# Six more q and k transposes on the DMA queue, and a new order of loads, in a fused attention and feed-forward kernel

## Chip, cores and metric

One NeuronCore of a Trainium2 chip. The metric is the device time of one execution in microseconds; the median of several runs is compared.

## The reference

```python
# q, k, v: (4 batches, 8 heads, 768 tokens, 64); n_sink = 4, window = 128
scores = q @ k.T / sqrt(64)
keep = (key position < n_sink) | (0 <= query position - key position < window)
a = softmax(where(keep, scores, -1e9))
x = (a @ v) with the heads side by side           # (3072 tokens, 512)
out = ((x @ w1) * (x @ w2)) @ w3 @ w_out          # 512 -> 1024 -> 1024 -> 512, float32 out
```

## The kernel before

The 3072 tokens are four batches of 768; each batch is six blocks of 128 tokens, in two halves ("chunks") of three blocks. Matrix products run in bf16 with float32 sums.

Since nothing nonlinear stands between w3 and w_out, the kernel first multiplies these two into one matrix w3o ("the fold"): TensorE transposes w3 (L349 and L380), and multiplies by w_out (L357 and L387). The first three row blocks of w3 are folded together, the other five one by one.

Attention for a batch goes through these steps. Loads bring q, k and v in by blocks of 128 tokens, 128 KB each, issued by GpSimd, which turns float32 into bf16 on the way (L159). q and k must stand with the head dimension on the partitions, so they are transposed into qkT, which has two buffers, one for even and one for odd batches. For batch 0 and batch 1 TensorE transposes (L437 and L460), into a PSUM tile mm, and ACT or DVE copies it to qkT (L142). For batches 2 and 3 the DMA engines transpose, issued by SP (L484), one instruction for one block of q or of k. Then TensorE computes scores (L585, and L523 for the four sink tokens), ACT takes the exponential (L603), DVE multiplies by a mask (L609), TensorE multiplies by v (L661, tile av), and DVE divides by the sum of weights (L671 and L676), into xs. xs is transposed once more into xT: on TensorE for batches 0 and 1 (L697), by DMA for batches 2 and 3 (L717).

The feed-forward part runs by halves of 384 tokens. For each of eight column blocks there are two gate products of four matmuls each (L741, one with w1 and one with w2, 384 columns), a copy of the first (L142, a_sb) and a multiplication with the second (L756, ab). Then the product with w3o (L771), a copy to o_sb (three buffers), and a store of 128 rows (L788, issued by SP).

The program's order is set at build time by a planner in the kernel (L792 on). Each step is an Op with an engine, an assumed duration, dependencies and a priority; the planner takes for each engine the step that can start soonest, and among those that can start at once the one with the lowest priority number. `when` (L425) gives attention steps their priority from LEAD and SPREAD; FOLD_J and FOLD_I give that of the fold. Idle places that the planner sees on TensorE in the first 45 us are filled with matmuls on zeros (L850, 104 of them). On the chip each engine then runs its own list strictly in this order, and waits only on semaphores. GpSimd takes the loads in the order of the string LOADS (L241), with eight outstanding at most.

The buffer `big` holds w3 and w_out, and later q and k of batches 2 and 3; so those loads come after the fold. The planner further orders the loads of batch 3 behind transposes of batch 2 and behind one another; DEEP says how many of them may be ahead. What it orders so on GpSimd is a place in time in the plan, not a semaphore on the chip. In SP's list, transposes of batch 3 stand behind those of xs of batch 2, by ORDER (L472).

Memory of PSUM: two wide tiles sc for scores, one av, three mm. The mm tiles serve gate products, output products and the transposes on TensorE alike.

Of the kernel before, what the change touches and what calls it, by code (L numbers as in the profile page):

```python
# [21 lines left out]
def kernel(  # L22
# [23 lines left out]
    NP = H // 2  # L46
    NB = S // P
    NC = 2
    QC = NB // NC
# [32 lines left out]
    qN = {0: early[0], 1: near[0]}  # L82
    kN = {0: early[1], 1: near[1]}
    for b in (2, 3):
        o = (b - 2) * 2 * NQ
# [36 lines left out]
    TUS = 1.3  # L122
# [14 lines left out]
    PE, ACT, DVE, POOL, SP = "pe", "act", "dve", "pool", "sp"  # L137
# [3 lines left out]
    def copy(out, in_):  # L141
        (nc.scalar.copy if turn_of[0] == ACT else nc.vector.tensor_copy)(out, in_)  # L142

    def cols(n, k=1):
        return k * (n / 2400.0 + 0.0025)

    def act_us(n):
        return 0.165 + n / 1200.0

    def dve_us(n, x=1.0):  # L150
        return 0.15 + n / 960.0 / x
# [12 lines left out]
    def pool_op(us, fn, deps=()):  # L164
        return Op(POOL, us, fn, deps)

    KA, LEAD, SPREAD = 3, 0, 0.9
    FOLD_J, FOLD_I = 0.5, 1010
    DEEP, ORDER = 2, 1
    FUSED = (1, 2, 3)  # L170
    KINDS = (0, 2, 2, 2)
    QK_BY_DMA = (2, 3)
    X_BY_DMA = ((2, 0), (2, 1), (3, 0), (3, 1))

    def load_w3(i):
# [15 lines left out]
    def load_qk(dst, src, b, c, h0, h1):  # L191
        return load(POOL, dst[b][:, c, h0:h1, :],
                    src[b, h0:h1, c * TOK:(c + 1) * TOK, :].rearrange("h (p j) d -> p h (j d)", j=QC),
                    (h1 - h0) * TOK * D * 4, QC * D * 4)
# [35 lines left out]
    got = {}  # L230
# [5 lines left out]
    for r in range(2):  # L236
# [2 lines left out]
            got["kq"[n], 0, 0, r] = cast((DVE, ACT)[n], 0.5, dst[0][:, 0, 2 * r:2 * r + 2, :],  # L239
                                         first_home[i][:, 0:TOK].rearrange("p (h m) -> p h m", h=2), st[i])  # L240
    LOADS = """k0-0-4 v0-0 ident q0-0-4 pick w3j-2-4 v0-1 tri v0-2 w3j-0-1 w3j-4-6 w3j-1-2 wo-1-2 wo-0-1  # L241
        wo-2-4 w3j-6-8 wo-4-6 w3-6 wo-6-8 w3-5 w3-4 q0-1-0 w3-7 k0-1-0 v0-5 w0 v0-3 v0-4 w3 k1-5
        q1-3 w2 w1 k1-4 w3-3 q1-1 k1-3 q1-4 q1-0 q1-5 k1-2 q1-2 v1-4 k1-0 q2-1 k1-1 q2-0 q2-2 k2-1
        q3-5 q2-3 v1-2 v1-1 v1-0 k2-2 k2-0 v2-4 v1-5 v2-0 k2-3 q3-2 v2-1 v1-3 v3-1 q2-5 v2-2 k2-5
        q2-4 k2-4 q3-4 k3-3 v3-2 v3-3 k3-5 v3-5 v3-0 v2-5 q3-3 k3-2 k3-4 v2-3 k3-1 q3-0 k3-0 v3-4
        q3-1"""

    def masks(part):
        m = maskt[:, 0, :].rearrange("p (k q) -> p k q", q=P)
# [27 lines left out]
    for key in LOADS.split():  # L277
        n = [int(x) for x in key[2 if key[:2] == "wo" else 3 if key[:3] == "w3j" else 1:].split("-") if x.isdigit()]
# [10 lines left out]
        elif key[:2] == "wo" or key[:3] == "w3j":  # L289
            o = (load_wo if key[1] == "o" else load_w3j)(*n)  # L290
# [13 lines left out]
        elif key[0] in "kq":  # L304
            _, c, h0 = n
            o = load_qk(kN if key[0] == "k" else qN, k if key[0] == "k" else q, 0, c, h0, h0 + (H if c else H // 2))
# [14 lines left out]
    def transposed(home_ap, n):  # L321
        return home_ap[:].bitcast(BF16)[:, 0:n]
# [8 lines left out]
    acc_keys, n = [], 0  # L331
# [80 lines left out]
    xt_ready, chunk_dep = {}, {}  # L412
# [3 lines left out]
    for b in range(B):  # L416
        kind = KINDS[b]
        T = qkT_home[b % 2]
        war = []
        if b >= 2:  # L420
            war = list(all_sc[b - 2])
        tp_of = {}
        base = 10 * b

        def when(part, early):  # L425
            return 1000 + 200 * (b - 1) + LEAD + 200 * SPREAD * part if b else early
        if b == 0:
            for c in range(NC):
                for r in range(NP):
                    x = []  # L430

                    def tps(b=b, c=c, r=r, x=x):
                        tp = transposed(x[0].slot["mm"], 6 * P).rearrange("p (s j m) -> p s j m", s=2, m=P)
                        for s, src in ((0, kN[b]), (1, qN[b])):
                            for j in range(QC):
                                for e in range(2):
                                    nc.tensor.transpose(tp[64 * e:64 * e + 64, s, j, :],  # L437
                                                        src[:, c, 2 * r + e, j * D:(j + 1) * D], ident[:])

                    def tpc(T=T, c=c, r=r, x=x):  # L440
                        tp = transposed(x[0].slot["mm"], 6 * P).rearrange("p (s j m) -> p s j m", s=2, m=P)
                        for s in range(2):
                            copy(
                                T[:, r, s, c * TOK:(c + 1) * TOK].rearrange("p (m j) -> p m j", j=QC),
                                tp[:, s, :, :].rearrange("p j m -> p m j"))
                    a = Op(PE, cols(P, 6) + 0.12, tps, [got["k", b, c, r], got["q", b, c, r], op_ident],
                           base + 1 + r * 0.1, takes=["mm"])
                    x.append(a)
                    tp_of[c, r] = Op(EITHER, (2 * act_us(3 * P), 2 * dve_us(3 * P)), tpc, [a],
                                     base + 1, frees=[(a, "mm")])  # L450
        elif b not in QK_BY_DMA:
            for c in range(NC):
                for r in range(NP):
                    x = []

                    def tps(b=b, c=c, r=r, x=x):
                        tp = transposed(x[0].slot["mm"], 6 * P).rearrange("p (s j m) -> p s j m", s=2, m=P)
                        for s, src in ((0, kN[b]), (1, qN[b])):
                            for j in range(QC):
                                nc.tensor.transpose(tp[:, s, j, :],  # L460
                                                    src[:, QC * c + j, r * P:(r + 1) * P], ident[:])

                    def tpc(T=T, c=c, r=r, x=x):
                        copy(
                            T[:, r, :, c * TOK:(c + 1) * TOK],
                            transposed(x[0].slot["mm"], 6 * P).rearrange("p (s m) -> p s m", s=2))
                    a = Op(PE, cols(P, 6), tps,
                           [got[n, b, QC * c + j] for n in "kq" for j in range(QC)] + [op_ident] + war,
                           when((r / 4 + c) / 2 - 0.1 if kind != 1 else r / 4 + c / 50 - 0.1, 0), takes=["mm"])
                    x.append(a)  # L470
                    tp_of[c, r] = Op(EITHER, (act_us(6 * P), dve_us(6 * P, 2)), tpc, [a], base + 1, frees=[(a, "mm")])
        if ORDER and b == 3 and 2 in QK_BY_DMA:  # L472
            for c in range(NC):
                if (2, c) in X_BY_DMA:
                    for (s_i, kb), o in tp_of.items():
                        if kb // QC == c:
                            o.after = chunk_dep[2, c][1][-1]
        if b not in QK_BY_DMA:
            tdep = lambda c, r: [tp_of[c, r]] + ([tp_of[0, r]] if c else [])
        else:  # L480
            for kb in range(NB):
                for s, n, src in ((0, "k", kN), (1, "q", qN)):
                    def dmt(b=b, s=s, src=src, kb=kb, T=T):
                        nc.sync.dma_start_transpose(out=T[:, :, s, kb * P:(kb + 1) * P], in_=src[b][:, kb, :])  # L484
                    tp_of[s, kb] = Op(SP, TUS, dmt, [got[n, b, kb]] + war, base)
                    tp_of[s, kb].turn, tp_of[s, kb].pitch = 1.1, TUS
            if b + 1 in QK_BY_DMA:
                seen = []
                for o in in_big:
                    if o.batch == b:  # L490
                        seen.append(next(t for t in tp_of.values() if o in t.deps))
                    elif o.batch == b + 1:
                        o.deps += seen[:-3]
                behind = [o for o in in_big if o.batch == b + 1]
                for o, p in zip(behind[DEEP:], behind):
                    o.deps.append(p)
            tdep = lambda c, r: [tp_of[s, kb] for s in range(2) for kb in range(3 * c + 3)]

        def sk(b=b, T=T):
            for e in range(2):  # L500
# [16 lines left out]
        for q0, q1 in groups:  # L517
# [21 lines left out]
            o = Op(ACT, act_us(w), sse, [a], base + 2, frees=[(a, "mm")])  # L539
# [22 lines left out]
        for n_v, visit in enumerate(visits):  # L562
# [26 lines left out]
            if sinks:  # L589
                sinks[2].append(s_)  # L590
                o = Op(ACT, act_us(sinks[3]), sinks[1], [s_], base + 2, frees=[(s_, "mm")])
# [237 lines left out]
    with tc.manual_schedule():  # L829
        left, lanes = len(ops), []  # L830
        while left:
# [5 lines left out]
            start, e, o = min(moves, key=lambda x: (x[0], x[1]))  # L837
# [4 lines left out]
            if e == PE and start < 45.0 and start - free[PE] > 0.12:  # L842
                one = cols(P) * (2 if free[PE] < WARM else 1)
                n = min(24, int((start - free[PE] - 0.05) / one))
# [9 lines left out]
            for i, n in enumerate(o.takes):  # L854
                f, s = rings[n].soonest()
# [74 lines left out]
```

## Time and profile before

| | us |
|---|---|
| median of four runs | 200.03 |
| the runs | 199.15, 200.17, 204.35, 199.89 |
| the profiled execution | 199.15 |
| its span, first to last instruction | 197.4 |
| TensorE busy | 192.3 |
| VectorE (DVE) busy | 112.0 |
| ScalarE (ACT) busy | 103.8 |
| GpSimd (POOL) busy, nearly all of it issuing loads | 73.1 |
| mean TensorE clock granted | 1.0 |

The page gives the busy time of each engine, then the span in 40 slices of some 4.9 us: a digit is the busy share in tenths. The chain of waits follows the last instruction back to what released it. Rows of groups give line, engine, operation, output <- input, number, and the shortest, median and longest duration in ns. In rows by time the columns are start, duration, engine, line, operation and count; several instructions that follow one another are put together in one row. In rows by stretches, the busy time of PE, the weight loads (PEld), DVE, ACT and POOL follow the length, then the granted clock, a DMA share and GB/s. DMA issued by SP shows there with the time it takes SP, not with the time until its data has landed.

### The profile page before, as it was taken

To read this page: it belongs to the slowest core of one execution; us is meant where nothing else is said; L and a number is where in the kernel's file an instruction comes from. 1 tells how busy PE (TensorE), PEld (TensorE's weight loads), DVE (VectorE), ACT (ScalarE), POOL (GpSimd) and SP (SyncE) were. 2 spreads that over 40 slices of the span, in tenths; PEclk is the share of its full clock that TensorE was granted. 3 is DMA by queue.
4 is the path that set the end of the run, shared out by engine and by line. 5 is a ranking of instruction groups with operands and counts; after the bars stand their busy time and mean duration, and the time that the engine had idled before them with its cause. 6 is when DMAs were issued, how large, how long until landed. Compare 5 with 4: busy or idle time off the path is not lost.

```text
span 197.4 us, 4573 instructions
## 1 busy us (share of the span) xinstructions
PE 192.3 (97%) x1840; PEld 118.0 (60%) x1840; DVE 112.0 (57%) x255; ACT 103.8 (53%) x165; POOL 73.1 (37%) x96
## 2 busy tenths in 40 slices
PE   7999999999999999999999999999999999999993
PEld 6776656567566546566665546654666665555442
DVE  3976507696356757866897704544698654223200
ACT  3683548754539567837456623335884433343233
POOL 7997547677998556535363000000000000000000
PEclk9999999999999999999999999999999999999999
DMA  6999999999999999999999965351202142020133
GB/s 173 173 184 193 202 190 183 181 193 165 155 154 138 155 181 183 207 167 185 142 155 157 139 180 178 67 107 56 106 3 45 34 134 56 2 106 3 53 129 137
DMA packets 98181, 26.42 MB, mean 134 GB/s; under 512 B 86896, under 2 KB 94576, under 8 KB 98160
## 3 DMA queue, kind: packets, MB, share of 16 engines
q0 software_dynamic: 73584, 14.29, 91.4%
q1 hardware_dynamic: 23888, 11.38, 26.4%
q10 hardware_dynamic: 688, 0.46, 0.7%
q8 instruction: 14, 0.23, 0.5%
q14 instruction: 7, 0.06, 0.1%
HBM read 29.39 MB, written 6.29 MB: 181 GB/s over the span
## 4 chain that ended last, share of the span: by engine, by line
PE 92%; DMA 3%; POOL 2%; ACT 1%; issue 1%; DVE 0%; POOLq 0%; DVEq 0%
PE mm L741 43%; PE mm L771 21%; PE av L661 8%; PE sc L585 6%; PE mm L387 4%; DMA big<-in_moe_w_dram 3%; PE sc L357 2%; PE mm L460 1%; PE mm L697 1%; PE mm L380 1%; PE mm L357 1%; PE mm L523 1%; POOL early L159 1%; PE mm L349 1%; PE av L850 1%
## 5 line engine op out<-in xcount | busy, mean ns | idle before, releaser
L741 PE MATMUL mm<-xT,w_sb 128*128 128x384 bf16 x512 | 90.3, 326 | 0.0
L741 PEld LDWEIGHTS <-w_sb 128*128 128x128 bf16 x512 | 47.7, 98 | 31.4 <-issue 1.8
L756 DVE TENSOR_TENSOR ab<-a_sb,mm 128x384 bf16<-128x384 f32 x64 | 35.4, 553 | 32.2 <-PE mm L741 27.7
L603 ACT ACTIVATE ex<-sc 128x1024 bf16<-128x1024 f32 (+2 forms) x49 | 44.0, 941 | 5.9 <-PE sc L585 4.3
L771 PE MATMUL mm<-w3o,ab 128*128 128x512 bf16 (+2 forms) x208 | 45.0, 363 | 0.0
L142 ACT COPY a_sb<-mm 128x384 f32<-128x384 f32 x53 | 25.3, 478 | 36.1 <-PE mm L741 18.2
L609 DVE TENSOR_TENSOR am<-ex,maskt 128x1024 bf16<-128x1024 bf16 (+2 forms) x49 | 30.1, 623 | 4.7 <-ACT ex L603 4.5
L771 PEld LDWEIGHTS <-ab 128*128 128x128 bf16 x208 | 18.8, 98 | 19.0 <-issue 0.6
L142 ACT COPY o_sb<-mm 128x512 f32<-128x512 f32 (+2 forms) x21 | 11.4, 545 | 25.7 <-PE mm L771 25.7
L159 POOL DMA_DIRECT2D vN<-in_v_dram x24 | 21.1, 884 | 6.8 <-DMA big<-in_k_dram 3.5
L661 PEld LDWEIGHTS <-am 128*128 128x128 bf16 x352 | 17.0, 97 | 3.5 <-issue 0.3
L661 PE MATMUL av<-vN,am 128*128 128x65 bf16 x352 | 19.0, 194 | 0.0
L676 DVE TENSOR_TENSOR xs<-av,rec 128x384 bf16<-128x384 f32 x32 | 17.7, 554 | 0.6
L671 DVE RECIPROCAL rec<-av 128x6 f32<-128x6 f32 x32 | 6.2, 194 | 16.6 <-PE av L661 16.4
L585 PE MATMUL sc<-qkT 64*128 64x128 bf16 (+1 forms) x248 | 14.7, 241 | 0.1
L159 POOL DMA_DIRECT2D big<-in_k_dram x12 | 10.6, 880 | 9.9 <-PE mm L741 2.9
L661 PE MATMUL av<-vsb,es 128*128 128x130 bf16 x64 | 12.9, 220 | 0.0
L159 POOL DMA_DIRECT2D big<-in_q_dram x12 | 10.6, 882 | 4.5 <-DMA vN<-in_v_dram 2.1
L585 PEld LDWEIGHTS <-qkT 64*128 64x128 bf16 x248 | 8.1, 94 | 5.9 <-issue 4.3
L387 PE MATMUL mm<-big,w3t 128*128 128x512 bf16 x40 | 9.5, 380 | 0.0
L850 PEld LDWEIGHTS <-zeros 128*128 128x128 bf16 x104 | 7.7, 115 | 2.0 <-DVE zeros L219 1.3
L850 PE MATMUL mm<-zeros 128*128 128x128 bf16 x75 | 7.4, 266 | 1.3 <-DVE zeros L219 1.3
(64 smaller groups left out, 143.8 us busy)
## 6 DMA issues: line engine op xcount, KB each, us to landing
out_dram<-o_sb SPq DMA_DIRECT2D x23, 256.0 KB
vN<-in_v_dram POOLq DMA_DIRECT2D x24, 128.0 KB, 10.6
w_sb<-in_moe_w_dram POOLq DMA_DIRECT2D x8, 256.0 KB, 9.8
big<-in_q_dram POOLq DMA_DIRECT2D x12, 128.0 KB, 7.8
big<-in_k_dram POOLq DMA_DIRECT2D x12, 128.0 KB, 10.5
big<-in_moe_w_dram POOLq DMA_DIRECT2D x5, 256.0 KB, 8.9
big<-in_moe_w_out_dram POOLq DMA_DIRECT2D x3, 256.0 KB, 6.4
near<-in_k_dram POOLq DMA_DIRECT2D x6, 128.0 KB, 7.9
```

Of the source, the lines that this page charges most:

```text
L142: (nc.scalar.copy if turn_of[0] == ACT else nc.vector.tensor_copy)(out, in_)
L159: op = Op(eng, us, lambda: (nc.gpsimd if eng == POOL else nc.sync).dma_start(out=out, in_=in_), deps)
L387: nc.tensor.matmul(x[2].slot["mm"][:], x[1].slot["w3t"][:, j, :], wo_sb[:, j, :], start=(j == 0), stop=(j == KFF - 1))
L585: nc.tensor.matmul(sc[:, e, c * P:(c + n) * P], T[hp, r, 0, kb * P:(kb + 1) * P], T[hp, r, 1, qb * P:(qb + n) * P], start=True, stop=True)
L603: nc.scalar.activation(y[1].slot["ex"][:, :, 0:w], y[0].slot[key][:, :, 0:w], ACTF.Exp, scale=scale)
L609: nc.vector.tensor_mul(y[2].slot["am"][:, :, 0:w], y[1].slot["ex"][:, :, 0:w], maskt[:, :, m0:m0 + w].to_broadcast([P, 2, w]))
L661: nc.tensor.matmul(o, lhs, rhs, start=(i == 0), stop=(i == len(todo) - 1), skip_group_check=True)
L676: nc.vector.tensor_mul(xs_first[c].slot["xs"][:, :, r * P:(r + 1) * P].rearrange("p k (e d) -> p k e d", d=D), av_of(x[0].slot["av"])[:, : ...
L741: nc.tensor.matmul(pg[:, 0:TOK], w_sb[:, kk, dt * P:(dt + 1) * P], holder[0].slot["xT"][:, kk, :], start=(kk == 0), stop=(kk == NP - 1))
L756: nc.vector.tensor_mul(abh[0].slot["ab"][:, dt, :], y[1].slot["a"][:], y[2].slot["mm"][:, 0:TOK])
L771: nc.tensor.matmul(x[0].slot["mm"][:, 0:n1 - n0], abh[0].slot["ab"][:, kk, mi * P:(mi + 1) * P], w3o[:, kk, n0:n1], start=(kk == 0), stop= ...
L850: nc.tensor.matmul(view, zeros[:], zeros[:], start=True, stop=True)
```

## The change

- Which transposes of q and k go to DMA is now given by batch and half. To both halves of batches 2 and 3, the second half of batch 1 is added. `tdep`, which says what a score must wait for, is made to fit halves of either kind. X_BY_DMA, which says the same for xs, is left as it is.
- DEEP goes from 2 to 3.
- LEAD goes from 0 to -200, SPREAD from 0.9 to 0.7: attention steps of a batch have the priority of a feed-forward half that lies one batch earlier, and lie closer together.
- FOLD_J goes from 0.5 to 50: the first, joint part of the fold comes after the attention steps of batch 0 that are ready. FOLD_I goes from 1010 to 1000.
- ORDER goes, and what it switched stays on, for the transposes by DMA only.
- The loads stand in a new order from the eighteenth on.

```diff
-    KA, LEAD, SPREAD = 3, 0, 0.9
-    FOLD_J, FOLD_I = 0.5, 1010
-    DEEP, ORDER = 2, 1
+    KA, LEAD, SPREAD = 3, -200, 0.7
+    FOLD_J, FOLD_I = 50, 1000
+    DEEP = 3
...
-    QK_BY_DMA = (2, 3)
+    QK_BY_DMA = ((1, 1), (2, 0), (2, 1), (3, 0), (3, 1))
     X_BY_DMA = ((2, 0), (2, 1), (3, 0), (3, 1))
...
-        wo-2-4 w3j-6-8 wo-4-6 w3-6 wo-6-8 w3-5 w3-4 q0-1-0 w3-7 k0-1-0 v0-5 w0 v0-3 v0-4 w3 k1-5
-        q1-3 w2 w1 k1-4 w3-3 q1-1 k1-3 q1-4 q1-0 q1-5 k1-2 q1-2 v1-4 k1-0 q2-1 k1-1 q2-0 q2-2 k2-1
-        q3-5 q2-3 v1-2 v1-1 v1-0 k2-2 k2-0 v2-4 v1-5 v2-0 k2-3 q3-2 v2-1 v1-3 v3-1 q2-5 v2-2 k2-5
-        q2-4 k2-4 q3-4 k3-3 v3-2 v3-3 k3-5 v3-5 v3-0 v2-5 q3-3 k3-2 k3-4 v2-3 k3-1 q3-0 k3-0 v3-4
-        q3-1"""
+        wo-2-4 w3j-6-8 wo-4-6 w3-6 wo-6-8 w3-5 q0-1-0 k0-1-0 w0 w2 v0-4 v0-3 v0-5 w3-3 k1-3 k1-4
+        w3 w1 v1-2 q1-3 w3-4 k1-1 w3-7 k1-0 k1-2 q1-2 v1-4 v1-3 k1-5 q1-4 q1-1 k2-2 q1-0 q1-5 v1-1
+        v2-4 k3-3 v1-0 k2-0 q2-2 k2-4 q3-2 q2-1 v1-5 k2-1 q2-0 q3-5 k2-5 v3-5 v2-1 k2-3 q2-5 v2-2
+        q2-4 v2-0 v3-3 q2-3 k3-4 v3-1 q3-4 v3-0 q3-0 k3-5 v2-3 v2-5 k3-2 q3-3 q3-1 k3-0 k3-1 v3-4
+        v3-2"""
...
-        elif b not in QK_BY_DMA:
+        else:
             for c in range(NC):
-                for r in range(NP):
+                for r in range(NP) if (b, c) not in QK_BY_DMA else ():
...
+        turned = {}
+        if any((b, c) in QK_BY_DMA for c in range(NC)):
             for kb in range(NB):
-                for s, n, src in ((0, "k", kN), (1, "q", qN)):
+                for s, n, src in ((0, "k", kN), (1, "q", qN)) if (b, kb // QC) in QK_BY_DMA else ():
                     def dmt(b=b, s=s, src=src, kb=kb, T=T):
                         nc.sync.dma_start_transpose(out=T[:, :, s, kb * P:(kb + 1) * P], in_=src[b][:, kb, :])
-                    tp_of[s, kb] = Op(SP, TUS, dmt, [got[n, b, kb]] + war, base)
+                    turned[s, kb] = Op(SP, TUS, dmt, [got[n, b, kb]] + war, base)
...
+        def tdep(c, r, b=b, tp_of=tp_of, turned=turned):
+            return sum(([turned[s, kb] for s in range(2) for kb in range(3 * c_, 3 * c_ + 3)]
+                        if (b, c_) in QK_BY_DMA else [tp_of[c_, r]] for c_ in range(c + 1)), [])
```

In LOADS, k1-3 is block 3 of k of batch 1, w3-4 row block 4 of w3, w2 columns 512 to 767 of both gate matrices.

More of the change, by code (lines that the diff above doesn't have):

```diff
@@ L471 @@
                     tp_of[c, r] = Op(EITHER, (act_us(6 * P), dve_us(6 * P, 2)), tpc, [a], base + 1, frees=[(a, "mm")])
[L472 to L480, printed above, removed]
+        turned = {}
+        if any((b, c) in QK_BY_DMA for c in range(NC)):
             for kb in range(NB):
-                for s, n, src in ((0, "k", kN), (1, "q", qN)):
+                for s, n, src in ((0, "k", kN), (1, "q", qN)) if (b, kb // QC) in QK_BY_DMA else ():
                     def dmt(b=b, s=s, src=src, kb=kb, T=T):
                         nc.sync.dma_start_transpose(out=T[:, :, s, kb * P:(kb + 1) * P], in_=src[b][:, kb, :])
-                    tp_of[s, kb] = Op(SP, TUS, dmt, [got[n, b, kb]] + war, base)
-                    tp_of[s, kb].turn, tp_of[s, kb].pitch = 1.1, TUS
-            if b + 1 in QK_BY_DMA:
+                    turned[s, kb] = Op(SP, TUS, dmt, [got[n, b, kb]] + war, base)
+                    turned[s, kb].turn, turned[s, kb].pitch = 1.1, TUS
+            if b == 2:
                 seen = []
@@ L490 @@
                     if o.batch == b:
-                        seen.append(next(t for t in tp_of.values() if o in t.deps))
+                        seen.append(next(t for t in turned.values() if o in t.deps))
                     elif o.batch == b + 1:
@@ L496 @@
                     o.deps.append(p)
-            tdep = lambda c, r: [tp_of[s, kb] for s in range(2) for kb in range(3 * c + 3)]
+        if b == 3:
+            for c in range(NC):
+                if (2, c) in X_BY_DMA:
+                    for (s_i, kb), o in turned.items():
+                        if kb // QC == c:
+                            o.after = chunk_dep[2, c][1][-1]
+        def tdep(c, r, b=b, tp_of=tp_of, turned=turned):
+            return sum(([turned[s, kb] for s in range(2) for kb in range(3 * c_, 3 * c_ + 3)]
+                        if (b, c_) in QK_BY_DMA else [tp_of[c_, r]] for c_ in range(c + 1)), [])
         def sk(b=b, T=T):
```

## Prediction

> **What bounds the kernel now.** I read the busy times and the 40 slices first, then the chain of waits, then busy time by stretches of 10 us.
>
> ```profile
> PE 192.3 (97%) x1840; PEld 118.0 (60%) x1840; DVE 112.0 (57%) x255; ACT 103.8 (53%) x165; POOL 73.1 (37%) x96
> ...
> PE   7999999999999999999999999999999999999993
> ...
> DMA  6999999999999999999999965351202142020133
> ...
> PE 92%; DMA 3%; POOL 2%; ACT 1%; issue 1%; DVE 0%; POOLq 0%; DVEq 0%
> ```
>
> ```profile
> 80.00:90.00 10.00, 10.00 (x107) 6.09 (x106) 7.35 (x16) 5.62 (x10) 5.24 (x6) 1.00 1.74 187
> ...
> 100.00:110.00 10.00, 10.00 (x97) 5.83 (x95) 8.83 (x18) 6.42 (x9) 3.86 (x5) 1.00 2.30 147
> ```
>
> TensorE is busy 10.00 of every 10 us from 20 to 190, at full clock, and the chain is 92% TensorE. Busy PE need not be dense PE, so I check the rate: the chain has 8 gate matmuls of 384 columns in 1.30 us (0.1625 each) and 8 of 512 columns in 1.73 (0.216 each), which is 2.37 columns per ns. So the program behind 10 us is one dense stream of matmuls. A matmul taken out shortens the run by its own time, and any wait that comes in lengthens it by all of its time, since nothing later can make it up.
>
> The second resource is the DMA engines: 9 tenths busy until slice 23, so until some 113 us. They carry the loads and the transposes.
>
> ```profile
> 74.92 2.32 SPq L788 DMA_DIRECT2D out_dram<-o_sb  x2
> 77.33 4.48 SPq L484 DMA_TRANSPOSE qkT<-big  x3
> 81.91 3.23 SPq L788 DMA_DIRECT2D out_dram<-o_sb  x2
> 85.23 10.26 SPq L484 DMA_TRANSPOSE qkT<-big  x6
> ```
>
> This is SP's queue by time. It is one line of transposes and output stores in a fixed order, some 1.24 us of SP per transpose. Following each transpose to its DMA semaphore in the trace, it lands 7.35 to 8.51 us after its issue for all issues from 56 to 94 us; from 112 us on, with the loads gone, 2.4 to 2.5 us (one 3.5).
>
> **What the Trainium skill says.** "TensorE: Matmul & The Clock Gate", section "Wait — 56ns, not 53.3ns?", gives 55.8 ns from start to start for 128 columns at full clock; the trace has six transposes in 0.34 us, 56.7 ns. "DMA: Bandwidth & Descriptors", section "Queues, rings and completion order", says that each DMA engine goes round robin between queues at packet granularity; this agrees with a transpose issued at 77.33 that lands at 85.84, while a load issued at 76.65 lands at 89.92. The same page, "Issuing engines are not separate DMA queues", says that all queues share the same 16 engines, so a transpose must cost load time; I measure that below. "VectorE: DVE Perf Modes", section "The three transpose paths", has 1309 ns for a 128x128 transpose by DMA; here 128x512 takes SP 1.24, so I use the trace.
>
> **Part 1: 24 matmuls go.** QK_BY_DMA now names (1, 1), so the transposes on PE (L460) for the second half of batch 1 are not made.
>
> ```profile
> L460 PE MATMUL mm<-ident,near x48: 216/219/219, 52.6 to 62.0; 128*128 128x128 bf16 x48
> ```
>
> ```profile
> 56.78 0.34 PE mm L460 x6
> ```
>
> 24 of 48 go: 24 x 0.0567 = 1.36 us off a saturated engine. Their four copies to qkT (0.80 each on ACT, or 0.56 on DVE) go too; these engines are 53% and 57% busy, so that is worth nothing by itself. The words of the change also name the attention output of this half, but the diff leaves X_BY_DMA alone: the changed instruction order still has all 48 transposes of xs. So 12 more matmuls, 0.68 us, are not saved. The 104 filler matmuls on zeros are 104 in both.
>
> **Part 2: six transposes come in on SP.** Each is 1.24 us of SP. They stand in order ahead of the first output store, and they wait for the loads of batch 1. SP is idle from 6 to 56 us. Behind them stand the first output stores (L790 in the changed file), due near 65, which free the three o_sb buffers; a late transpose would hold those, and through them the copies out of mm. The first scores to read them come late enough: in the changed order the loads of that half stand at places 28 to 49 of 87; load 49 of before lands at 59.05. With 2.5 us for three transposes in front of it, and 7.5 for the transpose of q block 5, it is there at some 70; the scores that read it start near 75. No wait. What they cost is load time. In the trace eight loads of 128 KB land in 7.37 us without a transpose beside them (0.92 each), and thirteen in 16.0 us (57.76 to 73.75) with five transposes landing: (16.0 - 12.0) / 5 = 0.8 us of load time for each.
>
> **Part 3: the last transpose for the first half of batch 2 (q block 0).** LEAD and SPREAD move attention forward, and the order puts this transpose behind the store of block row 4 of batch 0. So it hangs on TensorE itself. From the end of that row's projection: a copy to o_sb on DVE, with a reciprocal and a normalisation ahead of it in the queue, 0.69 to 1.3; the store on SP, 0.43 (76.91 to 77.33 in the trace); landing 7.35 to 8.5. Sum 8.5 to 10.2. Over the same stretch PE has 28 gate matmuls (4.55), 8 of 512 columns (1.73), 12 x-transposes (0.68), 30 av matmuls (1.1), the scores (some 0.7) and four changes between full and half tiles at 0.1: 9.0 to 9.1. So the wait is between none and 1.2; I take 0.45. Behind it on PE, which runs in order, stands everything.
>
> **Part 4: the last transpose for the second half (q block 3).** Its load is number 72. Load 72 of before lands at 94.26, with 12 transposes and 6 stores landed by then. In the changed order 16 transposes and 6 stores come before it: 4 x 0.8 later, some 97.5. The transpose lands 7.4 to 8.2 later, 104.9 to 105.7. TensorE reaches the first scores of batch 2 near 87.1 by the same count of the matmuls that stand ahead of them (81.28 in before, where less stands ahead), and from there has 80 gate matmuls (13.0), 63 av (2.3), scores and 6 transposes (1.6): 16.9. With the wait of part 3 that is 104.5. The wait is 0.4 to 1.2 by these numbers. Load 72 can be off by 1.5 us either way, so the bounds are 0 and 2.7; I take 0.65.
>
> **Part 5: the rest.** FOLD_J = 50 puts the first weight fold behind batch 0's attention at the start. That can remove the 0.4 us that L349 waits for its weights near 10 us, but brings two av groups together on the single av buffer, whose release takes a reciprocal (0.19) and a normalisation (0.55). I take 0, bounds -0.4 and +0.4. Near 85 us an x-transpose now stands between two gate groups on the three mm buffers: 0 to 0.4, I take 0.15. Batch 3's loads "three deep" is an ordering constraint of the plan, not a semaphore, and costs nothing; its transposes run after the loads have ended, with landings of 2.5 us. If loads did reach past 118 us, each would cost the 5 us more that a loaded landing takes.
>
> **The sum.** -1.36 + 0.45 + 0.65 + 0.15 = -0.1 us. The profiled execution took 199.15 (span 197.4, 1.75 around it), so some 199.05. It was the lowest of four; the median is 200.03, 0.9 above it. I put the same -0.1 on the median: 199.9.
>
> **The rivals.**
> Likeliest, 0.46: the saving is eaten by two short waits for transposes, 199.9, itself within 199.0 and 201.0.
> Rival A, 0.27: the landings are at the early bounds and PE sees no wait. Then -1.36 + 0.15 = -1.2: 198.8. For it: in before the last transpose for the same scores landed at 98.19, 0.7 ahead of their start, and no wait shows; loads may come sooner. Against it: the chain of part 3 has no spare time in the middle of its bounds.
> Rival B, 0.27, slower: the load queue with six more transposes in it delivers batch 2's second half late. The mechanism is part 4 alone: with load 72 at 99.1 the transpose lands near 107, a wait of 2.3, and the sum is -1.36 + 0.15 + 0.45 + 2.3 = +1.5: 201.6. It decides for slower once the waits together pass 2.2 us (1.36 - 0.15 + 1.0). For it: loads landed 1.74 us apart between 76 and 102 us. Against it: stores are not added, and loads of batch 2 stand earlier in the list.
>
> **Numbers.** 0.5%, 1.0 us, is about what a measurement can tell from no change. Faster by more: rival A, 0.27. Within: 0.46. Slower: rival B, 0.27. The range reaches to both: 198.5 (A with the start's 0.4 gained) to 201.9 (B with the start's 0.4 lost, less a little).
>
> **What would show it.** Part 1: L460 x24, PE busy less by some 1.4. Parts 3 and 4: scores (L587) waiting for a transpose qkT<-big near 87 and near 104 us, 0.3 to 1 us each; none of either means A, one over 2 us means B. Part 2: no wait of L587 on qkT<-near. I am wrong if PE waits somewhere before 80 us by more than 0.5, or if transposes land in much other than 7.4 to 8.5 us while loads run.

## Result and the profile after

The changed kernel takes 200.84 us (median of 35 runs, 199.48 to 203.98) where the kernel before takes 200.32 (56 runs on the same chips). The ratio is 1.005, with a 95% interval of 1.0034 to 1.0066: slower by 1.0 us. The medians take in runs in a slower state of the chip, of which the kernel before has more, and the ratio leaves them out, so it shows more than the medians' 0.3%. The forecast was 199.9, no change that can be measured. The two profiled executions lie further apart than the medians, 201.16 against 199.15, with spans of 199.5 and 197.4: that of before is one of its faster ones and that of after is near the middle.

The page of the changed kernel, the lines that answer to those shown of before (busy times, the 40 slices, the chain of waits):

```profile
PE 191.4 (96%) x1816; PEld 116.8 (59%) x1816; DVE 111.6 (56%) x254; ACT 100.6 (50%) x162; POOL 73.1 (37%) x96
...
PE   7999899997999999988999999999999999999994
...
DMA  6999999999999999999999998655520425010124
...
PE 68%; DMA 20%; POOL 8%; issue 1%; DVE 1%; SPq 0%; ACT 0%; POOLq 0%
```

TensorE has 24 instructions and 0.9 us of busy time less, as the diff says. But it now has slices below 9 where, the first and the last aside, it had none (slices 4, 9, 17 and 18, counted from 0, which is near 22, 49 and 85 to 95 us), and the chain that was 92% TensorE is 68%, with 20% DMA in it. The DMA engines are full for longer. By stretches of 10 us:

```profile
40.00:50.00 10.00, 8.77 (x84) 5.56 (x83) 6.85 (x15) 3.77 (x7) 4.32 (x7) 1.00 1.82 159
80.00:90.00 10.00, 8.90 (x97) 5.54 (x95) 8.61 (x19) 5.28 (x7) 3.49 (x4) 1.00 1.63 180
90.00:100.00 10.00, 9.46 (x101) 6.12 (x102) 7.42 (x16) 6.40 (x9) 7.18 (x9) 1.00 2.64 156
100.00:110.00 10.00, 10.00 (x96) 6.37 (x94) 5.76 (x14) 4.71 (x8) 5.54 (x7) 1.00 2.05 134
```

The second column is TensorE: 1.23 us are missing between 40 and 50, 1.64 between 80 and 100, and none from 100 to 110, where the forecast had put its largest wait. What TensorE waited for in the kernel before (total, times, longest), all of it:

```profile
PE mm L850 <- DVE zeros L219: 1.3, 1, 1.3
PE mm L349 <- DMA big<-in_moe_w_dram: 0.4, 1, 0.4
```

And in the changed kernel:

```profile
PE sc L587 <- DMA qkT<-big: 1.6, 1, 1.6
...
PE mm L380 <- DMA big<-in_moe_w_dram: 1.2, 1, 1.2
PE sc L357 <- DMA big<-in_moe_w_out_dram: 0.7, 1, 0.7
```

The three waits for DMA shown end at 90.54, 49.91 and 22.71 us. Ends of matmuls are modelled, so I also take the distance between the starts of adjacent matmuls, less the time of the first at 2.4 columns per ns (the dense stretches before gave 2.37), and call it the gap: 1.81, 1.40 and 0.84 us. The first is the first scores of batch 2 waiting for the transpose of q block 0; the second is the transposes of w3 row 4, for the weight fold, waiting for their load. The chain through both, in order of time (start, length, what):

```profile
38.53 11.34 DMA big<-in_moe_w_dram
...
49.91 0.62 PE mm L380 x8
...
78.80 0.88 PE mm L773 x4
...
79.70 0.69 DVE o_sb L142
...
81.61 0.32 SPq L790
...
82.02 8.48 DMA qkT<-big
...
90.54 0.61 PE sc L587 x8
```

And SP's queue at that place:

```profile
78.02 0.55 SPq L790 DMA_DIRECT2D out_dram<-o_sb  x1
78.67 2.60 SPq L477 DMA_TRANSPOSE qkT<-big  x2
81.36 0.56 SPq L790 DMA_DIRECT2D out_dram<-o_sb  x1
82.02 1.27 SPq L477 DMA_TRANSPOSE qkT<-big  x1
```

The copy to o_sb ends at 80.39, and its store could go then. SP is still at two transposes (2.60 us), so the store goes at 81.36 and the transpose that the scores wait for at 82.02.

### The profile page after: what moved, and what is told of

It reads as the page before. It is cut to its first block, busy times and chain, and to the rows that moved or that the text cites. A ratio compares the mean times of both kernels' runs of the same rounds, so it can differ in the third digit from the quotient of the medians.

```text
span 199.5 us, 4524 instructions
## 1 busy us (share of the span) xinstructions
PE 191.4 (96%) x1816; PEld 116.8 (59%) x1816; DVE 111.6 (56%) x254; ACT 100.6 (50%) x162; POOL 73.1 (37%) x96
## 4 chain that ended last, share of the span: by engine, by line
PE 68%; DMA 20%; POOL 8%; issue 1%; DVE 1%; SPq 0%; ACT 0%; POOLq 0%
PE mm L743 34%; PE mm L773 20%; DMA big<-in_moe_w_dram 10%; DMA vN<-in_v_dram 6%; PE av L663 5%; DMA qkT<-big 4%; PE sc L587 4%; POOL big L159 4%; POOL vN L159 2%; PE mm L387 2%; POOL early L159 1%; PE mm L460 1%; PE mm L525 1%; PE mm L380 1%; DVE am L611 0%
## 5 line engine op out<-in xcount | busy, mean ns | idle before, releaser
L743 PE MATMUL mm<-xT,w_sb 128*128 128x384 bf16 x512 | 89.0, 326 | 0.0
L743 PEld LDWEIGHTS <-w_sb 128*128 128x128 bf16 x512 | 48.2, 98 | 31.6 <-issue 1.4
L587 PE MATMUL sc<-qkT 64*128 64x128 bf16 (+1 forms) x248 | 14.6, 240 | 1.6 <-DMA qkT<-big 1.6
L587 PEld LDWEIGHTS <-qkT 64*128 64x128 bf16 x248 | 8.1, 94 | 7.9 <-issue 4.0
L142 DVE COPY qkT<-mm 128x384 bf16<-128x384 bf16 (+1 forms) x11 | 5.7, 553 | 5.6 <-PE mm L437 3.3
```

The lines of the kernel that those rows point to most:

```text
L587: nc.tensor.matmul(sc[:, e, c * P:(c + n) * P], T[hp, r, 0, kb * P:(kb + 1) * P], T[hp, r, 1, qb * P:(qb + n) * P], start=True, stop=True)
L743: nc.tensor.matmul(pg[:, 0:TOK], w_sb[:, kk, dt * P:(dt + 1) * P], holder[0].slot["xT"][:, kk, :], start=(kk == 0), stop=(kk == NP - 1))
```

## Experiments

Every kernel was timed in turn with the kernel before on the same chip; the ratios below are to it, with 95% intervals, and the kernels of one group of four share its runs. Where the landing of a load is given, it was followed from its issue to its DMA semaphore in the trace. In the kernels marked "order of issue only" all engines have the same instructions as in their parent, and only the named ones stand at another place in their queue; in the others the planner makes the order anew, unless the text says that it is kept. Line numbers shift by one to eight.

| kernel | median us | ratio to before |
|---|---|---|
| changed, again | 202.09 | 1.0094 (1.0058 to 1.0130) |
| two transposes after the w3 load | 199.58 | 0.9949 (0.9925 to 0.9973) |
| k block 4 of batch 2 later | 200.44 | 1.0014 (0.9991 to 1.0038) |
| both moves | 199.38 | 0.9959 (0.9930 to 0.9988) |
| old numbers and loads, planned anew | 209.26 | 1.0443 (1.0396 to 1.0490) |
| new order, TensorE transposes | 200.04 | 0.9982 (0.9954 to 1.0011) |
| FOLD_J back | 204.41 | 1.0156 (1.0087 to 1.0225) |
| both moves, FOLD_J back | 201.63 | 1.0049 (1.0020 to 1.0078) |
| old plan, six DMA transposes | 205.90 | 1.0290 (1.0260 to 1.0321) |
| both moves, loads first | 197.94 | 0.9895 (0.9868 to 0.9921) |
| new order, two transposes added | 202.31 | 1.0099 (1.0068 to 1.0131) |
| both moves, w_out first | 198.68 | 0.9928 (0.9904 to 0.9952) |

**The changed kernel again.** No edit.

> The changed kernel once more, for a second profile. If the three waits of its first profile belong to the change, the two behind transposed data come back: the first scores of batch 2 (L587) wait 1 to 2 us near 90 us for the transposed q block 0, and the transposes of w3 row 4 (L380) wait 0.5 to 1.5 us near 50 us for their load. The third, L357 waiting 0.7 us near 22 us, lies ahead of everything that the change moves in the load queue; if it is an accident of that one execution it is under 0.3 us here. Time 1.003 to 1.007 of before.

Both waits are back: a gap of 1.93 us before L380 at 50.59, and of 1.63 before L587 at 91.04. So is that of L357, 0.75 at 22.60: it is no accident of one execution, and my expectation there was wrong. Over the first 30 us as a whole, though, the gaps add up to 3.7 us here and 4.0 in the first profile of the changed kernel, against 3.3 in the kernel before; in the other profiles with the new list of loads they are 2.6 to 4.3. The start explains little of the difference. The time, 1.0058 to 1.0130, overlaps the first measurement (1.0034 to 1.0066) only at its lower end, and its middle is above what I expected. So differences from the changed kernel, below, are uncertain by some 0.4% according to which of its two measurements is taken.

**Two transposes behind the w3 load** (order of issue only).

```diff
+                    turned[s, kb].tag = (b, s, kb)
...
+    LATE = {(1, 0, 3): (1, 1, 3), (1, 0, 4): (1, 1, 3)}
...
-            o.fn()
+            tag = getattr(o, "tag", None)
+            if tag in LATE:
+                held.append((LATE[tag], o.fn))
+            else:
+                o.fn()
+                for at, fn in held:
+                    if at == tag:
+                        fn()
```

LATE names an instruction by batch, 0 for k or 1 for q, and block, and after the colon the one behind which it is given out.

> The changed kernel with its first two DMA transposes (k blocks 3 and 4 of batch 1) given to SP after that of q block 3 (issued at 49.06 us) and no longer at 38.0 and 39.4. All else, the order of the loads included, stays. Theory (these two transposes share the DMA engines with the load of w3 row 4, which is needed first, and cost it about 0.8 us each): that load lands 1.0 to 1.6 us earlier, the wait of L380 near 50 us falls from 1.4 to below 0.4, and the time falls 0.5 to 1.4 us against the changed kernel: about 0.998 to 1.002 of before. Rival (the new order of the loads alone puts w3 row 4 too late): the wait stays at about 1.4 and the time at 1.003 to 1.007.

The load of w3 row 4 lands at 46.51 and no longer at 49.87; the wait of L380 is gone altogether, and that of the first scores is as it was:

```profile
PE sc L588 <- DMA qkT<-big: 1.8, 1, 1.8
```

Of the 3.36 us, 0.66 were there before the transposes began (k block 4 of batch 1 landed at 38.86 and at 38.20). So two transposes had cost that load 2.7 us, 1.35 each. The time went down by 1.0% of before, 2.0 us (by 1.4% against the changed kernel's second measurement, on the same chip), which is more than the gap of 1.4 us and more than expected; the excess I can't place. The theory holds in its mechanism, and the rival, the order of the loads alone, falls.

**One transpose of batch 2 behind the urgent one** (order of issue only).

```diff
+    LATE = {(2, 0, 4): (2, 1, 0)}
```

> The changed kernel with one DMA transpose (k block 4 of batch 2, which belongs to the second half and is used only after 104 us) given to SP after that of q block 0 of batch 2 (issued at 82.02 us, the one the first scores wait for) and no longer before it. Theory (SP works its queue off one by one, is busy without a gap from 71.9 to 85.5 us, and each transpose holds it 1.3 us): the transpose of q block 0 is issued about 1.3 us earlier, lands about 1.3 earlier, and the wait of L587 near 90 us falls from 1.8 to about 0.5; time 0.7 to 1.4 us less than the changed kernel, 0.998 to 1.002 of before. Rival (the issue waits for the store ahead of it, whose data are late, or the landing is set by the load queue): issue or landing move by less than 0.4 us and the wait stays above 1.4.

0.9991 to 1.0038 against 1.0034 to 1.0066 for the changed kernel: some 0.7 us better, at the low end of the theory; against the second measurement of the changed kernel it is 1.6 us, above the theory's upper end. Its profile is of an execution 1.5 us above its own median, so I don't read the waits from it, but from the next kernel.

**Both moves** (order of issue only).

```diff
+    LATE = {(1, 0, 3): (1, 1, 3), (1, 0, 4): (1, 1, 3), (2, 0, 4): (2, 1, 0)}
```

> Both moves of the two kernels before in one. Theory: the two waits are in series on TensorE and independent, so both go: time 1.6 to 2.8 us less than the changed kernel, 0.991 to 0.997 of before, which is faster than both kernels. Rival (a wait that goes at 50 us comes back at 90, since the work there is set by SP and the DMA engines and not by TensorE): the wait at 90 grows by what the one at 50 loses, and the time is that of the kernel with the second move alone.

```profile
PE sc L588 <- DMA qkT<-big: 0.7, 1, 0.7
```

```profile
75.04 2.61 SPq L477 DMA_TRANSPOSE qkT<-big  x2
78.35 0.34 SPq L791 DMA_DIRECT2D out_dram<-o_sb  x1
78.78 2.63 SPq L477 DMA_TRANSPOSE qkT<-big  x2
```

Against the kernel with the first move alone, the gap before the first scores goes from 1.94 to 0.84 us, and the wait gone at 50 us doesn't come back. SP now is free before the store; the store goes as soon as its data are there, and only the landing (78.78 to 87.36, 8.58 us) is left. The whole is faster than the kernel with the second move alone, as the theory had it. That it is also faster than the one with the first move alone (0.9925 to 0.9973) is not shown: the profile has 1.1 us less of gap, but the intervals of the two times cover each other.

**The DMA transposes with the old numbers** and with the LOADS of the kernel before, the plan made anew from them.

```diff
-    KA, LEAD, SPREAD = 3, -200, 0.7
-    FOLD_J, FOLD_I = 50, 1000
-    DEEP = 3
+    KA, LEAD, SPREAD = 3, 0, 0.9
+    FOLD_J, FOLD_I = 0.5, 1010
+    DEEP = 2
```

> One part of the change alone: the kernel before, its numbers and its order of loads (LEAD 0, SPREAD 0.9, FOLD_J 0.5, FOLD_I 1010, DEEP 2), with the second half of batch 1 turned by DMA. Theory (the 24 matmuls are a gain of 1.36 us, and what ate it are waits that come from the new order, which puts loads and transposes too close to their users): in the old order the w3 rows have landed by 28 us and all of batch 2's first half by 70 us, so neither the wait near 50 nor that near 90 us is there, and the time is 0.992 to 0.997 of before. Rival (six more transposes cost the load queue 1.3 us each, 8 us in all, whatever the order, and the second half of batch 2 waits near 105 us instead): that wait is 1 to 3 us and the time 0.999 to 1.006.

Neither theory: 4.4% slower. TensorE is busy for only 5.24 us between 80 and 90 us and for 7.49 of 8 between 90 and 98. It waits for exponentials on ScalarE (2.5 us), for normalised outputs on VectorE (2.1) and for transposed data (0.9), and its granted clock was 0.70 and 0.73 in these two stretches. The planner put batch 1's attention quite differently, so this is not the one part alone that I meant. I didn't follow it further; "the old plan with six DMA transposes", below, takes its place.

**The new order with TensorE's transposes.**

```diff
-    QK_BY_DMA = ((1, 1), (2, 0), (2, 1), (3, 0), (3, 1))
+    QK_BY_DMA = ((2, 0), (2, 1), (3, 0), (3, 1))
```

> The other part alone: the changed kernel with its numbers and its order of loads, but the second half of batch 1 turned by TensorE again (24 matmuls and four copies back, six DMA transposes gone). Theory (the wait near 50 us comes from the two early transposes, that near 90 us from SP's queue and from loads made late by them): L380 waits less than 0.4 us near 50, the first scores of batch 2 less than 0.8 near 90; against the changed kernel +1.36 - 1.4 - 1.0 to 1.8, which is 0.995 to 1.000 of before. Rival (the new order of the loads by itself makes both waits): they stay within 0.4 us of 1.4 and 1.8 and the time is 1.008 to 1.013.

All that TensorE waits for:

```profile
PE mm L852 <- DVE zeros L219: 1.3, 1, 1.3
PE sc L357 <- DMA big<-in_moe_w_out_dram: 0.6, 1, 0.6
PE mm L349 <- DMA big<-in_moe_w_dram: 0.3, 1, 0.3
```

Neither wait is there. The row of w3 lands at 47.05 and is used at 48.20; q block 0 of batch 2 lands at 70.85, where in the changed kernel it lands at 79.97. With the same list of loads, six transposes more make that load 9 us later. So the new list by itself makes neither wait. For the one near 50 us this is close to a test of the transposes alone, since the two plans have the same order on TensorE up to there. For the one near 90 us it is weaker: from some 51 us on the planner orders TensorE's work differently, and here the transposed q block 0 lands at 83.98, only 0.5 us before its scores start. What makes that wait is better seen in the kernels with moves on SP's queue. The list, with the plan that comes of it, is worth nothing measurable (0.9954 to 1.0011).

**FOLD_J back**, in the changed kernel, and in the one with both moves.

```diff
-    FOLD_J, FOLD_I = 50, 1000
+    FOLD_J, FOLD_I = 0.5, 1000
```

> The changed kernel with FOLD_J back at 0.5, so that the first weight fold stands where it stood before. Theory: the wait of L357 near 22 us (0.4 to 0.85 in the profiles of the changed kernel and of those with its plan) comes from the fold's new place, and goes; L349 waits 0.4 near 10 us again; the rest stays. Against the changed kernel -0.8 to 0, 1.000 to 1.005 of before. Rival (the load of the last rows of w_out lands late by chance, whatever the place of the fold): the wait stays and the time is the changed kernel's.

> The kernel with both moves on SP's queue (transposes of k blocks 3 and 4 of batch 1 after that of q block 3, that of k block 4 of batch 2 after that of q block 0), and FOLD_J at 0.5 as well. Theory: all three waits are smaller, so it is 0.3 to 0.8 us better than the kernel with both moves, 0.992 to 0.996 of before. Rival: the fold's place is worth nothing, and it is within 0.2 us of that kernel.

Both theories fall. L357 still waits 0.8 us at 22.6 in the first, none in the second; but the plan that this number gives has waits for transposed data at two places, near 90 us and some 18 us later (1.9 and 1.8 us in the first, 1.2 and 1.2 in the second), so both are slower than their parents. LEAD, SPREAD and FOLD_I, by contrast, do nothing once the rest is changed: with their old values the planner gives the same order of the instructions on all five engines.

**The old plan with six DMA transposes.** All as in the kernel before, but for what turns the second half of batch 1.

```diff
+    TURN = ((0, 4), (0, 5), (1, 3), (0, 3), (1, 4), (1, 5))
...
-                    def tps(b=b, c=c, r=r, x=x):
+                    def tps(b=b, c=c, r=r, x=x, T=T):
+                        if (b, c) == (1, 1):
+                            for s, kb in TURN if r == 0 else ():
+                                nc.sync.dma_start_transpose(out=T[:, :, s, kb * P:(kb + 1) * P],
+                                                            in_=(kN, qN)[s][b][:, kb, :])
+                            return
...
-                    def tpc(T=T, c=c, r=r, x=x):
+                    def tpc(T=T, b=b, c=c, r=r, x=x):
+                        if (b, c) == (1, 1):
+                            return
```

> The kernel before with its plan, its order of loads and every other instruction in place, but the 24 matmuls and four copies that turn the second half of batch 1 left out, and six DMA transposes put at the head of SP's queue in their stead (k blocks 4 and 5, q block 3, k block 3, q blocks 4 and 5, in the order in which their loads landed before, 45.6 to 52.9 us). Theory (the change of the plan, not the DMA transposes as such, made the waits): in the old order the w3 rows land by 28 us, and the first half of batch 2 has 5 us to spare, so nothing waits and the 1.36 us stay: 0.991 to 0.996 of before. Rival (six transposes cost the loads behind them up to 1.5 us each, 9 in all, wherever they stand): the scores of batch 2 wait 1 to 3 us for transposed data between 80 and 106 us, and the time is 0.998 to 1.006.

2.9% slower, worse than either theory had it:

```profile
PE mm L466 <- DMA near<-in_k_dram: 4.0, 2, 2.5
...
PE sc L593 <- DMA qkT<-big: 1.3, 1, 1.3
```

L466 is TensorE's own transposes of the first half of batch 1. The old list loads that half behind the second. Its last block, k block 1, landed at 56.96 in the kernel before, some 2 us ahead of its use (L460 from 58.9 on); with six transposes beside the loads it lands at 63.23. They are issued at 45.9 to 54.9 us. The gaps are 4.4 us there, and 1.4 at 106 us for transposed data of batch 2, which is the place that the rival named. A further gap of 0.8 us stands at 53 us, for a copy on ScalarE, and the granted clock was 0.87 from 60 to 65 us and 0.79 from 65 to 70, which by these figures is some 1.7 us more (an estimate). So my theory that the new plan made the waits is wrong. The same exchange, six transposes in and 24 matmuls out, costs the old plan 2.9%, and the new one, from 0.9982 to 1.005, 0.7%. So the new list of loads and the plan made from it suit the transposes better, though not well enough; which of the two does it was not tried apart.

**Two transposes added to the new order.** The parent is the kernel with TensorE's transposes.

```diff
             o.fn()
+            if getattr(o, "tag", None) == ("k", 1, 4):
+                for kb in (3, 4):
+                    nc.sync.dma_start_transpose(out=qkT_home[1][:, :, 0, kb * P:(kb + 1) * P], in_=kN[1][:, kb, :])
```

> The kernel with the new order of loads and the second half of batch 1 turned by TensorE (it measured 0.998 of before, its w3 row 4 landed at 47.05 us and was used at 48.20), with two DMA transposes added at the head of SP's queue, of k blocks 3 and 4 of batch 1; what they write is written once more by the copies of the TensorE transposes, so that they only cost time. They are issued near 38 us as in the changed kernel. Theory (a transpose takes 1.3 to 1.7 us of load time from loads that land beside it): w3 row 4 lands at 49.7 to 50.5, L380 waits 1.4 to 2.2 us, time 1.004 to 1.009 of before. Rival (the price of 0.8 us each that the profile before gave): it lands at 48.6, the wait is under 0.5 and the time 0.998 to 1.001.

```profile
PE mm L381 <- DMA big<-in_moe_w_dram: 1.7, 1, 1.7
```

The row of w3 lands at 50.58 (47.05 without them; k block 4, ahead of them, at 38.74 and 38.71). Two transposes that nobody needs cost 3.53 us of landing, 1.77 each, and bring the wait at 50 us back in a kernel that had none. The theory holds, with the landing and the time a little above their upper ends; this profile also has 0.9 us more of gaps in its first 30 us, ahead of the two transposes. A price of 0.8 for these two is out.

**Both moves, and three loads and a store put back.** Order of issue only.

```diff
+    LATE = {(1, 0, 3): (1, 1, 3), (1, 0, 4): (1, 1, 3), (2, 0, 4): ('o', 0, 5, 0), ('k', 3, 3): ('q', 2, 0), ('q', 3, 2): ('q', 2, 0), ('q', 3, 5): ('q', 2, 0), ('o', 0, 4, 0): (2, 1, 0)}
```

Here ('k', 3, 3) is the load of a block, k block 3 of batch 3, and ('o', 0, 4, 0) the store of row block 4 of batch 0.

> The kernel with both moves on SP's queue, and more done for the transpose of q block 0 of batch 2: three loads that belong to batch 3 (k block 3, q blocks 2 and 5) are given to the load queue after the load of that q block, so that it lands some 2.5 us earlier; on SP the transpose goes ahead of the store of row block 4, and that of k block 4 behind the store of row block 5. Theory (what is left of the wait near 88 us, 0.84, is SP's queue and the landing of that load at 78.4): the transpose is issued near 77.5 and no longer at 80, the wait goes, and the time is 0.990 to 0.995 of before. Rival (the wait only moves on: with the store late the o_sb buffers hold PE up, or batch 3 lands late): 0.994 to 0.999 and a new wait after 90 us.

```profile
75.46 3.96 SPq L478 DMA_TRANSPOSE qkT<-big  x3
79.52 1.50 SPq L792 DMA_DIRECT2D out_dram<-o_sb  x2
```

```profile
PE mm L856 <- DVE zeros L219: 1.3, 1, 1.3
PE sc L358 <- DMA big<-in_moe_w_out_dram: 0.7, 1, 0.7
PE mm L350 <- DMA big<-in_moe_w_dram: 0.2, 1, 0.2
```

The load of q block 0 lands at 73.97 (78.42 with the two moves alone). The urgent transpose is the third of the three, issued at 78.17 and landed at 85.24, 1.8 us ahead of its use. No transposed data and no w3 row are waited for any more, the late store holds nobody up, and no new wait comes after 90 us. The span is 195.9, 1.5 less than before's, and the time 1.05% less (0.79 to 1.32%), a little better than the theory's range. Against the kernel with the same list of loads and TensorE's transposes (0.9982), which waits for none of this either, it is 0.9% less, some 1.7 us. The 24 matmuls' 1.36 us are there when nothing eats them.

**The last rows of w_out ahead of w3 row 6**, with both moves. Order of issue only.

```diff
+    LATE = {(1, 0, 3): (1, 1, 3), (1, 0, 4): (1, 1, 3), (2, 0, 4): (2, 1, 0), 'w3-6': 'wo-6-8'}
```

> The kernel with both moves on SP's queue, and the load of the last two rows of w_out (wo-6-8) given to the load queue ahead of that of w3 row 6. Theory (the wait of L357 near 22 us, 0.4 to 0.85 in all profiles with the new order, is a wait for this load's landing): it lands 1.2 us earlier, that wait is under 0.2, and the time is 0.4 to 0.7 us less than without it, 0.992 to 0.995 of before. Rival (it waits for the weights' copies and evictions, or TensorE is given fillers there anyway and loses nothing): 0.995 to 0.998.

The time agrees with the theory, the trace doesn't: the load lands at 20.43, 1.5 us earlier, yet L357 has a gap of 0.60 near 22 us, and 0.60 without the edit, in both put down to a copy of w3t on VectorE. The gap before the first scores of batch 2 is 1.20 us here. The intervals (0.9904 to 0.9952, and 0.9930 to 0.9988 without it) overlap. What L357's gap near 22 us is made of stays open.

## Why the prediction was wrong

**Part 1, 24 matmuls go: right.** "24 of 48 go": the trace has 24 of L460. That they are worth 1.36 us is borne out by the kernel with both moves and three loads and a store put back: 1.5 us off the span, with the waits gone.

**Part 2, six transposes come in: the step that failed first.** It said "No wait. What they cost is load time", and (16.0 - 12.0) / 5 = 0.8 us for each. The cost was left there, as if nobody stood behind it. The forecast gave the waits before 80 us nothing, and they took 1.40 us near 50. I asked whether the scores of that half get their data in time, and they do (nothing waits on near). I did not ask which loads stand behind the transposes in time and when those are used. The first two, issued at 38.03 and 39.42, run beside the load of w3 row 4, whose user had some 1.1 us to spare in the same order without them. They made it late by 2.7 to 3.5 us, and the fold by 1.40. The price was also too low: it is 1.35 each by taking two away, 1.77 each by adding two, and about 1.0 each for six in the old plan (k block 1 is 6.27 us later there, of which 0.36 were there before the transposes began). The slope of 0.8 was read from loads and transposes that overlap only in part, in one trace. Why one figure differs from another I can't say.

**Part 3, the transpose of q block 0: the mechanism right, the size wrong.** The chain was named: projection of row block 4, copy, store, transpose, scores. TensorE's work over the stretch was put at 9.0 to 9.1 us (the terms given add up to 9.2); it is 9.05 (79.68 to 90.54, less the gap of 1.81). The sum of the chain was put at "8.5 to 10.2"; it is 10.82: copy 0.71, SP at earlier transposes 0.97, store 0.66, landing 8.48. What is missing is the second of these; the store also took 0.66 where I had 0.43, and the landing was at its upper bound. I took the store as going when its data are there, and its time from a place where SP was free. SP works its queue one by one and was busy without a gap from 71.9 to 85.5 us, one of its transposes (k block 4) belonging to a half that is used 17 us later. Taking that one out of the way took 1.1 us off the wait; putting the urgent one ahead of the store, with its load earlier, took the rest; these two were not tried apart. Nor did I ask when the load of q block 0 itself lands: at 79.97, so that with a landing of 8.48 even a free SP would have had the data there only 0.3 us before TensorE came to it. The landings of the kernel before run from 7.01 us, and not from 7.35 as I read them, which changes nothing here.

**Part 4, the transpose of q block 3: no wait, where I took 0.65.** Its load lands at 98.15 (I had 97.5), the transpose is issued at 98.16 and lands at 106.81 (I had 104.9 to 105.7), and TensorE gets to the scores at 107.55 (I had 104.5), because it has lost 3 us more on the way. The load's landing came out near by luck: 14 transposes had landed by then, two more than in the kernel before and not four, and it was 3.9 us later all the same. A wait upstream pays for one downstream; they don't add. With the upstream waits gone the data come earlier as well (104.19 in the kernel with both moves, 103.29 in the one with the loads and the store put back too), and there is no wait there either. With FOLD_J back, in another plan, there is one of 1.2 us. Rival B, which was to make the kernel slower, has the sign right and the place wrong.

**Part 5, the rest: about right.** The start is a wash within the scatter of the profiles. Near 85 us the mm buffers cost nothing. "LEAD and SPREAD move attention forward", in part 3, is wrong: with the rest changed they change nothing in the order, and what does is the rest. Whether DEEP costs anything by itself I didn't try.

**The sum.** -1.36, +1.40 near 50 us and +1.81 near 90 make +1.85, of the 2.1 us between the two spans; the start adds 0.7 (gaps of 4.0 us against 3.3) and the end, after the last matmul, takes 0.4 off. The forecast had -1.36 + 0.45 + 0.65 + 0.15: nothing at 50 us where there were 1.40, 0.45 near 90 where there were 1.81, and 0.65 near 105 where there was none. The ratio says +1.0 and not 2.1, since the profile before is one of the faster executions. I had said that I am wrong "if PE waits somewhere before 80 us by more than 0.5"; it did, by 1.40.

"Advanced Engine Details and Errata" in the Trainium skill, section "X-Bar Transpose (TRN2)", says that transposing DMAs are as fast as regular ones. Here a block's load takes 0.92 us of the queue, and a transpose of one such block took 1.0 to 1.8 us from the loads beside it. The measurement decides: beside loads a transpose is the dearer of the two here, by little to nearly twice.

## What to carry over

Work moved from a saturated engine to the DMA engines was paid here by the loads beside it. So list the loads that are in flight or queued while the new transfers run, with the time at which each is used, and subtract the price from each one's spare time. A queue that issues in order, as SP's did here, is to be counted like any other engine: count what stands ahead of the urgent item, and put items of later stages behind it. This change should have gained 1.36 us and lost 1.0; moving four issues on SP's queue and three loads was enough to get the gain back (0.9895 of before).

## What the runs showed of the hardware

A DMA transpose of a 128x512 block cost the loads beside it 1.0 to 1.8 us each, though TensorE does the same block's share of work in 0.23 us (four of 0.0567). While loads run it landed 7.0 to 8.5 us after its issue in the kernel before and 6.9 to 9.6 in the changed one, and from 130 us on, with the loads gone, 2.4 to 2.5 in the kernel before. It holds SP for 1.2 to 1.4 us mostly, but over 2 now and then (2.28 at 74.27 us in the changed kernel, 2.50 at 57.46 in the fastest), and an output store held SP for 0.33 to 0.56 in the changed kernel.
